# A spectral and dense block pair on one core: half of the filter rows by plain loads, x in six loads, and a new written order

## The chip, the core and the metric

The kernel runs on one core of a Trainium2 chip. The metric is the device time of one execution in microseconds; the kernel before was run three times, and its median is what a changed kernel is compared with. The profile is one execution, taken by the hardware profiler.

## What is computed

x has 2048 rows of 448 bf16 values. Two kinds of layer alternate, twice each. Layer A is a filter in frequency space; layer B is a dense layer with a squared ReLU. Both start from a layer norm and add to x:

```
def _A_ref(x, w_r, w_i):
    X = rfft2(x.astype(float32), axes=(-2, -1))
    X = X * (w_r + 1j * w_i)            # w_r, w_i: 2048 x 225
    return irfft2(X, s=(S, D), axes=(-2, -1)).astype(bfloat16)
def _B_ref(x, w1, b1, w2, b2):
    h = einsum("bsd,df->bsf", x, w1) + b1     # 448 -> 1792
    r = where(h > 0, h, 0)
    return einsum("bsf,fd->bsd", r * r, w2) + b2
x = x + _A_ref(_layernorm(x), A_w_r, A_w_i)
x = x + _B_ref(_layernorm(x), B_w1, B_b1, B_w2, B_b2)
x = x + _A_ref(_layernorm(x), A_w_r, A_w_i)
x = x + _B_ref(_layernorm(x), B_w1, B_b1, B_w2, B_b2)
```

## The kernel before

Row p*16 + t of x is partition p of tile t; there are 16 tiles of 128 x 448. The transform over the 2048 rows is split into 128 x 16, all as matmuls with constant tables:

- First stage (`first_A`, one call for each tile): a 128 x 256 table FA is scaled by the rows' 1/std into Fs (`scaled`, recorded at line 758, 760 or 762 by engine), five matmuls bring x, its mirror copy xr and the mean m2 through it, and an evacuation writes XA. xr is a reversed copy of half of each row, made by GpSimd or ACT (units "XR", line 744); it lies in the tile VT. The statistics come from `ln_stats` on VectorE (bn_stats at line 865, aggregate at 866), or, for the tiles in `ACT_STATS`, from two passes on ACT (`act_stats`, lines 887 and 888), then a square root on ACT and a reciprocal (896).
- Spectral stage (`spectral`): `stage_TD` takes the transform over the 448 columns (64 matmuls in the first layer), evacuated to U in `arena`; `stage_B` ("quad") ends the transform over the rows with the table G; its evacuation lands in EF, also in `arena`; `stage_W` multiplies with the filter Wt on VectorE (line 780, 16 products of 128 x 896, written to `wide`); `stage_Bi` ("row") starts the way back with the table H (256 matmuls, eight groups of 32) and is evacuated to VT.
- `ffn`: `stage_TI` and `stage_AI` end the way back (tables TI, FI); x is updated; `ln_B` prepares the layer norm; yT, the transposed input, comes by matmuls (`flip`) for tiles 0 and 1 and by a transposing DMA on SP for the other tiles, two at a time; `h_part` and `h_pairs` multiply with W1, `o_tile` with W2. Then `second_A` feeds the second spectral layer. All matmuls but the fillers are recorded at line 718; matmuls on `ones` at line 1375 are fillers that keep TensorE busy.

The filter tile Wt has four blocks of 16 x 225 values for each partition: rows of w_r and of w_i, and for both the mirrored rows that belong to the negative frequencies. Partition p holds in the first two blocks rows from 128*(p & 15) + 16*(p >> 5) + 1 on, 16 rows in one run of 7200 bytes. Before, all four blocks come by an indirect DMA on GpSimd's queue (`gather`, line 838), with row numbers that VectorE works out from an iota (`ints`, line 800). In GpSimd's list the two mirrored blocks are gathered first, early in the first stage; the two direct blocks (units 26 and 25) come near the end of the list, the one after the scaled tables of tiles 12 and 13, the other last before three fillers. Two small loads, tagged L.W0, write row 0 and its fellows over one row of partitions 96 to 127 of the mirrored blocks, so they need the mirrored gathers to have landed. A product needs all four blocks.

The program records units (a matmul group, an evacuation, a load) with numbers in the order in which they are created. `ORDER` holds, for each of the five engines, the list of its units in the order in which they are issued; every engine goes through its list in turn and waits for what its next unit needs. A load is a unit on the list of the queue that issues it, SP, ACT or GpSimd; a queue that waits for one unit issues nothing behind it. `_Sched.schedule` with the constants `DMA_FIRST`, `TURN`, `PACE` and so on is a model of the times; with a written ORDER it sets the filler matmuls, the banks of PSUM and on which side a wait is put, not the lists. Units that can run on ACT or VectorE run on that engine in whose list they stand.

Loads before, on SP in this order: x tile 0, FA, x tiles 2, 4, 6-7, 10-11, 14-15, TD, G, G0, the two halves of H (each waits until tile 11, or 13, of XA is evacuated), L.W0 twice, TI, FI, J, b1, b2, W1 in two loads (384 rows over 128 partitions, 64 rows over 64), b1 over two rows, TQ, W2, then the first transposing DMA. On ACT: x tiles 1, 5, 8-9, 3, 12-13.

Of the kernel before, what the change touches and what calls it, by code (L numbers as in the profile page):

```python
# [6 lines left out]
ALU = mybir.AluOpType  # L7
# [4 lines left out]
P = 128  # L12
# [21 lines left out]
def make_constants():  # L34
# [64 lines left out]

    H = np.zeros((P, 16, 2, 3, 16, 2, 2))  # L100
    for n in range(16):
        for j in range(4):
            kappa = 16 * j + n + 1
            for f in range(2):
# [10 lines left out]
                for k, M in enumerate((-s, c, s)):  # L115
                    H[32 * j:32 * j + 32, n, f, k, :, j % 2] = M
# [29 lines left out]
1275 1280 1247 1241 1291 1285 1288 1294 1297""",  # L146
    "act": """
# [11 lines left out]
1231 1179 1189 1184 1058 1187 1182 1253 1258 1256 1263 1261 1251 1266 1268 1271 1273 1276 1283 1281 1278""",  # L159
    "dve": """  # L160
# [22 lines left out]
1242 1286 1289 1295 1298""",  # L183
    "pool": """
16 0 30 28 27 46 29 31 33 54 32 34 35 109 37 99 112 36 96 26 151 138 135 25 19 17 18""",
    "sp": """
4 5 7 9 11 13 15 38 39 40 155 156 157 158 159 160 161 162 163 164 165 166 167 168 286 306 324 326 344 327 362 380 398
# [1279 lines left out]
```

## Time and profile before

| | |
|---|---|
| three runs | 259.51, 264.21, 259.23 us; median 259.51 |
| the profiled execution, its own time | 258.75 us |
| its span, first to last instruction | 257.0 us |
| granted TensorE clock | 1.000 |
| moved by DMA | 18.10 MB in 23936 packets |
| instructions | 6149, of these 2462 matmuls |

How to read it: a row of the timeline has start and duration in us, engine, line, operation, the tile that is written and the tiles that are read, how often it was repeated, and in brackets the idle time ahead of it with what ended it. A row of the groups has busy us and the mean ns of one. A row of the stages gives, for a stretch, the busy time of PE, PEld (weight load), DVE (VectorE), ACT (ScalarE) and POOL (GpSimd), the granted clock, the share of the 16 DMA engines that is busy, and GB/s. SPq and ACTq are the queues that issue loads. A row of DMA issues ends with KB and the us from issue to landing. The tile W_sb stands for W1_sb and W2_sb, since digits are left out of names.

### The profile page before, as it was taken

The numbers are of one execution on the slowest core, as the hardware profiler recorded it, in microseconds if no ns is written. First come the engines' busy times: TensorE is split into PE (matmuls) and PEld (weight loads), VectorE is DVE, ScalarE is ACT, GpSimd is POOL, SyncE is SP. The second block draws the span as 40 slices with busy tenths as digits, with TensorE's granted clock in tenths as the row PEclk, the third lists the DMA queues.
The fourth block names the chain that finished last, engine by engine and source line by source line (L and its number), as shares of the span: only waits on it lengthen the run. The fifth ranks groups of instructions, "written<-read, shape, count | busy, mean of one in ns | idle before, by whom it ended". The sixth has DMA issues, their size and how long they took to land.

```text
span 257.0 us, 6149 instructions
## 1 busy us (share of the span) xinstructions
PE 246.8 (96%) x2462; PEld 160.8 (63%) x2462; DVE 191.8 (75%) x628; ACT 168.5 (66%) x363; POOL 14.3 (6%) x31
## 2 busy tenths in 40 slices
PE   8799788999999999999999999999999999999995
PEld 2578577886544865544558778787645775545453
DVE  3994796999875759889999898999982288023732
ACT  5987888986467775207957898999368883018300
POOL 4890000000000000000000000000000000000000
PEclk9999999999999999999999999999999999999999
DMA  6989945011321000130000000022231021000025
GB/s 180 414 278 395 288 111 176 15 28 43 73 46 43 0 0 3 42 42 3 0 3 1 3 3 3 3 41 45 42 79 41 0 61 41 3 18 0 3 80 172
DMA packets 23936, 18.10 MB, mean 70 GB/s; under 512 B 15938, under 2 KB 22562, under 8 KB 23908
## 3 DMA queue, kind: packets, MB, share of 16 engines
q1 hardware_dynamic: 22612, 13.22, 18.6%
q0 software_dynamic: 576, 3.69, 3.7%
q10 hardware_dynamic: 720, 0.80, 1.0%
q8 instruction: 19, 0.31, 0.5%
q14 instruction: 9, 0.07, 0.1%
HBM read 12.20 MB, written 1.84 MB: 55 GB/s over the span
## 4 chain that ended last, share of the span: by engine, by line
PE 73%; DVE 11%; ACT 7%; DMA 6%; issue 2%; POOL 1%; SPq 0%; POOLq 0%; DVEq 0%
PE ps L718 72%; DMA Wt<-in_A_w_r_dram,ix 4%; ACT arena L743 3%; ACT VT L743 2%; DMA xin<-in_A_x_dram 2%; DVE arena L780 2%; DVE st L865 2%; DVE wide L780 1%; DVE x_sb L1228 1%; ACT arena L737 1%; PE ps L1375 1%; DVE VT L1107 1%; DVE x_sb L1082 1%; DVE Fs L758 1%; DVE wide L789 1%
## 5 line engine op out<-in xcount | busy, mean ns | idle before, releaser
L718 PE MATMUL ps<-wide,W_sb 64*128 64x512 bf16 (+1 forms) x770 | 90.1, 346 | 0.0
L718 PE MATMUL ps<-W_sb,arena 128*128 128x448 bf16 (+3 forms) x476 | 87.1, 342 | 0.0
L718 PEld LDWEIGHTS ps<-wide,W_sb 64*128 64x128 bf16 (+1 forms) x770 | 57.2, 95 | 29.3 <-issue 1.5
L737 ACT ACTIVATE arena<-ps,b1col 128x512 bf16<-128x512 f32 x84 | 52.2, 687 | 27.0 <-PE ps L718 26.8
L718 PEld LDWEIGHTS ps<-W_sb,arena 128*128 128x128 bf16 x476 | 45.5, 98 | 38.0 <-issue 0.4
L780 DVE TENSOR_TENSOR arena<-arena 128x512 bf16<-128x512 bf16 (+1 forms) x140 | 45.1, 365 | 24.5 <-ACT arena L737 24.4
L1106 ACT ACTIVATE VT<-x_sb 128x448 bf16<-128x448 bf16 x28 | 16.2, 581 | 13.3 <-DVE x_sb L1082 13.3
L743 ACT ACTIVATE arena<-ps 128x896 bf16<-128x896 f32 (+1 forms) x27 | 20.5, 828 | 3.7 <-PE ps L718 3.6
L780 DVE TENSOR_TENSOR wide<-arena,Wt 128x896 bf16<-128x896 bf16 x32 | 17.7, 617 | 1.9 <-DMA Wt<-in_A_w_r_dram,ix 1.9
L737 ACT ACTIVATE arena<-ps 128x256 bf16<-128x256 f32 x56 | 17.9, 400 | 1.8 <-PE ps L718 1.3
L737 ACT ACTIVATE mv<-mv,epst 128x1 f32<-128x1 f32 (+1 forms) x45 | 12.6, 294 | 9.4 <-DVE mv L866 8.1
L1228 DVE SCALAR_TENSOR_TENSOR x_sb<-ps,mv,xin 128x448 bf16<-128x448 f32 (+2 forms) x13 | 8.1, 643 | 14.1 <-PE ps L718 14.0
L718 PE MATMUL ps<-H_sb,wide 64*128 64x128 bf16 x512 | 16.2, 217 | 1.2 <-issue 1.2
L743 ACT ACTIVATE XA<-ps 128x512 bf16<-128x512 f32 (+1 forms) x28 | 14.3, 581 | 4.2 <-PE ps L718 4.1
L718 PEld LDWEIGHTS ps<-H_sb,wide 64*128 64x128 bf16 x512 | 14.4, 94 | 4.0 <-issue 2.2
L718 PE MATMUL ps<-wide,VT 64*128 64x512 bf16 x42 | 15.8, 377 | 0.0
L743 ACT ACTIVATE wide<-ps 128x896 bf16<-128x896 f32 (+3 forms) x19 | 13.9, 780 | 1.9 <-PE ps L718 1.9
L743 ACT ACTIVATE VT<-ps 128x1024 bf16<-128x1024 f32 (+1 forms) x16 | 12.7, 876 | 1.6 <-PE ps L718 1.5
L1375 PE MATMUL ps<-ones 128*128 128x512 bf16 (+2 forms) x32 | 10.3, 450 | 2.9 <-DVE m L879 1.3
L744 DVE CAST arena<-ps 128x896 bf16<-128x896 f32 (+1 forms) x11 | 9.3, 873 | 5.0 <-PE ps L718 5.0
L762 ACT ACTIVATE wide<-x_sb,rstd 128x448 bf16<-128x448 bf16 x12 | 8.1, 675 | 6.6 <-DMA wide<-wide 5.1
L1082 DVE SCALAR_TENSOR_TENSOR x_sb<-ps,mv,xin 128x448 bf16<-128x448 f32 x16 | 10.5, 678 | 0.4 <-PE ps L718 0.3
(83 smaller groups left out, 277.7 us busy)
## 6 DMA issues: line engine op xcount, KB each, us to landing
out_dram<-x_sb SPq DMA_DIRECT2D x15, 112.0 KB, 1.8
W_sb<-in_B_w_dram SPq DMA_DIRECT2D x1, 1568.0 KB, 8.1
H_sb<-c_H SPq DMA_DIRECT2D x2, 768.0 KB, 8.1
W_sb<-in_B_w_dram SPq DMA_DIRECT2D x1, 1344.0 KB, 11.3
xin<-in_A_x_dram SPq DMA_DIRECT2D x3, 224.0 KB, 5.6
G_sb<-c_G SPq DMA_DIRECT2D x1, 512.0 KB, 10.7
xin<-in_A_x_dram ACTq DMA_DIRECT2D x2, 224.0 KB, 5.0
VT<-in_B_w_dram SPq DMA_DIRECT2D x2, 192.0 KB, 3.1
```

The source lines that it names most:

```text
L718: return sch.add("pe", lambda e: e.matmul(_res(o), lhsT, rhs, start=start, stop=stop, skip_group_check=skip), [lhsT, rhs], [o], cost=cost, ...
L737: sch.add("act", lambda e: e.activation(o, _res(i), func, **kw), rd, [o], cost=c)
L743: op = sch.add(engs[0], lambda e: e.activation(o, _res(i), ACT.Copy) if h[0].eng == "act" else e.tensor_copy(o, _res(i)), [i], [o], cost=c ...
L744: e.tensor_copy(o, _res(i)), [i], [o], cost=c[engs[0]], unit=unit)
L758: return e.tensor_scalar(o, i, s, 1.0, op0=ALU.mult, op1=ALU.mult)
L762: op = sch.add(engs[0], lambda e: e.activation(o, i, ACT.Copy, scale=s) if h[0].eng == "act" else scale(e), [i, s], [o], cost=c[engs[0]])
L780: sch.add(eng, lambda e: e.tensor_tensor(o, _res(a), b, op), [a, b], [o], cost=_free(o) / rate + 69.0)
L865: small(lambda e, si=si, xi=xi: e.bn_stats(si, xi), [xi], [si], _free(xi) / 0.96 + 69.0)
L1082: small(lambda e, xx=xx, xi=xi, r=r, m=m: e.scalar_tensor_tensor(out=xx, in0=_res(r), scalar=m, in1=xi, op0=ALU.subtract, op1=ALU.add), [r ...
L1106: op = sch.add("act", lambda e, i=i, o=o, x=x, h=h: e.activation(o, x, ACT.Square, accum_out=sd[:, i, 1:2]) if h[0].eng == "act" else e.sc ...
L1228: small(lambda e: e.scalar_tensor_tensor(out=o, in0=_res(i), scalar=rs[0] if rs else 1.0, in1=xi, op0=ALU.add if t >= 4 and last else ALU. ...
L1375: return lambda e: e.matmul(ps[:, b, 0:n], ones[:], ones[:, None, :].to_broadcast([P, n // P, P]), start=True, stop=True)
```

## The change

1. Two gathers instead of four. The direct blocks of the filter come by eight plain loads on SP, one for each of four groups of 32 partitions and each of w_r, w_i, behind G0. For this partition p now holds the rows of (p & 30) >> 1 instead of p & 15, and the tables G, G0 and H are permuted alike (`by`); the two L.W0 loads have a source of [16 rows][2][225] instead of [2][16 rows][225].
2. The two halves of H no longer wait for XA: they follow the plain filter loads at once.
3. x comes in six loads instead of eleven: tiles 0, 4-7 and 12-15 on SP, 1, 2-3 and 8-11 on ACT.
4. Tiles 3 and 5 get their statistics on VectorE; tiles 2-3 and 4-5 are groups of two. Only tile 1 stays with ACT.
5. New lists for all engines, and other constants in the model.

There are six units fewer ahead of the spectral stage, so a unit that was number n is now n - 6 from old number 171 on. Some units of the new lists: 11 ones, 12 the filler memset of W1, 0 iota, 19 and 20 the gathers (w_r, w_i), 21 to 29 the mirror copies of tiles 0, 1, 2-3, 4-5, 6-7, 8-9, 10-11, 12-13, 14-15; 64, 67, 77, 90, 93, 103, 106, 129, 132, 119, 142, 145 the scaled tables of tiles 2, 3, 4, 6, 7, 8, 9, 12, 13, 11, 14, 15; 30 to 32 TD, G, G0; 33 to 40 the plain filter loads; 149 and 150 H; 151 and 152 L.W0; 153 to 159 TI, FI, J, b1, b2, W1; 160 b1 over two rows; 280 the first transposing DMA; 161 TQ; 162 W2.

```diff
+    by = [16 * r + k for k in range(16) for r in range(2)]
+    G, G0 = (M.reshape(M.shape[:-1] + (2, 32))[..., by].reshape(M.shape) for M in (G, G0))
...
-                    H[32 * j:32 * j + 32, n, f, k, :, j % 2] = M
+                    H[32 * j:32 * j + 32, n, f, k, :, j % 2] = M[by]
...
     "pool": """
-16 0 30 28 27 46 29 31 33 54 32 34 35 109 37 99 112 36 96 26 151 138 135 25 19 17 18""",
+11 12 0 23 20 21 24 29 25 67 64 90 93 77 28 27 103 106 129 132 13 119 142 145 19 14""",
     "sp": """
-4 5 7 9 11 13 15 38 39 40 155 156 157 158 159 160 161 162 163 164 165 166 167 168 286 306 324 326 344 327 362 380 398
...
+4 5 8 10 30 31 32 33 34 35 36 37 38 39 40 149 150 151 152 153 154 155 156 157 158 159 160 280 161 162 300 318 320 338
...
-A1GROUPS = ((0, 1), (1, 1), (2, 1), (3, 1), (4, 1), (5, 1), (6, 2), (8, 2), (10, 2), (12, 2), (14, 2))
-ACT_STATS = (1, 3, 5)
+A1GROUPS = ((0, 1), (1, 1), (2, 2), (4, 2), (6, 2), (8, 2), (10, 2), (12, 2), (14, 2))
+ACT_STATS = (1,)
...
-    DMA_FIRST = 3500.0
-    TURN = 100.0
+    DMA_FIRST = 2900.0
+    TURN = 93.0
...
+    FETCH = (94, 128, 4300.0)
...
-        row = ((0, 2, 15, ALU.bitwise_and, 7, ALU.logical_shift_left), (1, 2, 5, ALU.logical_shift_right, 4, ALU.logical_shift_left))
+        row = ((0, 2, 30, ALU.bitwise_and, 6, ALU.logical_shift_left), (1, 2, 5, ALU.logical_shift_right, 4, ALU.logical_shift_left))
...
-        for a, n, q in ((0, 1, "sp"), (1, 1, "act"), (2, 1, "sp"), (3, 1, "act"), (4, 1, "sp"), (5, 1, "act"), (6, 2, "sp"),
-                        (8, 2, "act"), (10, 2, "sp"), (12, 2, "act"), (14, 2, "sp")):
+        for a, n, q in ((0, 1, "sp"), (1, 1, "act"), (2, 2, "act"), (4, 4, "sp"), (8, 4, "act"), (12, 4, "sp")):
             dma(q, xin[:, a:a + n, :], x_dram[:, a:a + n, :])
...
-        ints(ix[:, 0:1], ix[:, 2:3], 1, ALU.bitwise_or, 0, ALU.bitwise_or)
-        ints(ix[:, 1:2], ix[:, 2:3], 2032, ALU.bitwise_xor, 0, ALU.bitwise_or)
+        ints(ix[:, 0:1], ix[:, 2:3], 2032, ALU.bitwise_xor, 0, ALU.bitwise_or)
...
         for w in range(2):
-            gather(0, w, WS * w, 16)
-        sch.tag = "M2"
-        for w in range(2):
-            gather(1, w, WS * (2 + w), 16)
+            gather(w, WS * (2 + w), 16)
...
         dma("sp", G0_sb[:], dc["G0"])
+        for j in range(4):
+            for w, a in enumerate((A_w_r, A_w_i)):
+                sch.tag = f"L.W.{j}.{w}"
+                dma("sp", Wt[32 * j:32 * j + 32, WS * w:WS * (w + 1)],
+                    bass.AP(a.tensor, a.offset + (16 * j + 1) * (LW + 1), [[P * (LW + 1), 16], [0, 2], [1, WS]]))
...
-            dma("sp", H_sb[:, 8 * i:8 * i + 8], dc["H"][:, 8 * i:8 * i + 8], after=[XA[:, 0, 0, 0, 11 + 2 * i, 0:1]])
+            dma("sp", H_sb[:, 8 * i:8 * i + 8], dc["H"][:, 8 * i:8 * i + 8])
         for w, a in enumerate((A_w_r, A_w_i)):
             sch.tag = f"L.W0.{w}"
             dma("sp", Wt[96:128, WS * (2 + w):WS * (2 + w) + LW + 1],
-                bass.AP(a.tensor, a.offset, [[0, 2], [P * (LW + 1), 16], [1, LW + 1]]))
+                bass.AP(a.tensor, a.offset, [[P * (LW + 1), 16], [0, 2], [1, LW + 1]]))
```

More of the change, by code (lines that the diff above doesn't have):

```diff
@@ L136 @@
     "pe": """
[9 rows of a table removed]
-1275 1280 1247 1241 1291 1285 1288 1294 1297""",
-    "act": """
[11 rows of a table removed]
-1231 1179 1189 1184 1058 1187 1182 1253 1258 1256 1263 1261 1251 1266 1268 1271 1273 1276 1283 1281 1278""",
-    "dve": """
[22 rows of a table removed]
-1242 1286 1289 1295 1298""",
[9 rows of a table added]
+1274 1235 1241 1232 1282 1279 1285 1288 1291""",
+    "act": """
[11 rows of a table added]
+1252 1255 1257 1262 1250 1260 1272 1277 1270 1267 1275 1265""",
+    "dve": """
[22 rows of a table added]
+1283 1280 1286 1289 1292""",
     "pool": """
-16 0 30 28 27 46 29 31 33 54 32 34 35 109 37 99 112 36 96 26 151 138 135 25 19 17 18""",
+11 12 0 23 20 21 24 29 25 67 64 90 93 77 28 27 103 106 129 132 13 119 142 145 19 14""",
     "sp": """
-4 5 7 9 11 13 15 38 39 40 155 156 157 158 159 160 161 162 163 164 165 166 167 168 286 306 324 326 344 327 362 380 398
-948 969 987 989 990 1007 1025 1043 1152 1061 1193 1243 1155 1293 1199 1196 1202 1240 1146 1149 1290 1287 1246 1249
-1296 1299""",
+4 5 8 10 30 31 32 33 34 35 36 37 38 39 40 149 150 151 152 153 154 155 156 157 158 159 160 280 161 162 300 318 320 338
+321 356 374 392 942 963 981 983 1001 984 1143 1140 1019 1037 1055 1240 1149 1190 1193 1237 1243 1234 1281 1284 1287
+1146 1196 1187 1290 1293""",
 }
@@ L400, in schedule @@
         begun = [0.0] * self.DEEP
-        sent = 0.0
+        sent, block = 0.0, 0.0
         def supply(start):
-            nonlocal sent
+            nonlocal sent, block
             sent = max(sent + self.PACE, begun[-self.DEEP])
+            if (len(begun) - self.DEEP) % self.FETCH[1] == self.FETCH[0]:
+                block = sent = max(sent, block + self.FETCH[2])
             start = max(start, sent)
@@ L433, in ready_of @@
                             same = d.eng == u.eng and not d.is_dma
-                            r = max(r, done[d] + d.lat + (40.0 if u.eng == "pe" else 0.0) - off)
+                            r = max(r, done[d] + (50.0 if d.is_dma and d.cost != 1000.0 else d.lat) + (40.0 if u.eng == "pe" else 0.0) - off)
                     off += op.cost
@@ L469, in schedule @@
         total = len(self.units)
-        mode = "full"
+        mode, turn = "full", self.TURN
         avail = {}
@@ L487, in schedule @@
                         if u.mode != mode:
-                            f += self.TURN
+                            f += turn
                     starts.append((max(r, f), u))
@@ L530, in schedule @@
                     free["pe"] += unit
-                start = max(start, free["pe"] + (self.TURN if u.mode != mode else 0.0))
+                start = max(start, free["pe"] + (turn if u.mode != mode else 0.0))
                 mode = u.mode
@@ L566, in schedule @@
             if e == "pe":
+                turn = self.TURN + u.ops[-1].lat - 200.0
                 used.append((start, t))
@@ L711, in dma @@
                 w = min(run(o), run(i))
-                sch.add(eng, fn, reads, writes, is_dma=True, cost=450.0 if o.tensor.name not in onchip else 550.0, lat=n / w * (7.5 + 2.0 * w / 27.0) / 16.0 * (2.0 if writes and _parts(o) == 64 else 1.0))
+                sch.add(eng, fn, reads, writes, is_dma=True, cost=460.0, lat=n / w * (7.5 + 2.0 * w / 27.0) / 16.0 * (2.0 if writes and _parts(o) == 64 else 1.0))
         def mm(o, lhsT, rhs, start, stop, skip=False, unit=None):
@@ L815, in bass_interleave_layers__spectral_gfnet__dense_activation_squared_relu__prompt_kernel @@
         act(warm[:, 0:1], warm[:, 0:1], ACT.Sqrt)
+        sch.units[-1].ops[0].cost = 1300.0
         sch.table_deps = [sch.last_write[k] for k in _pages(warm[:, 0:1])][:1]
-        for a, n, q in ((0, 1, "sp"), (1, 1, "act"), (2, 1, "sp"), (3, 1, "act"), (4, 1, "sp"), (5, 1, "act"), (6, 2, "sp"),
-                        (8, 2, "act"), (10, 2, "sp"), (12, 2, "act"), (14, 2, "sp")):
+        for a, n, q in ((0, 1, "sp"), (1, 1, "act"), (2, 2, "act"), (4, 4, "sp"), (8, 4, "act"), (12, 4, "sp")):
             dma(q, xin[:, a:a + n, :], x_dram[:, a:a + n, :])
@@ L832, in bass_interleave_layers__spectral_gfnet__dense_activation_squared_relu__prompt_kernel, with gather @@
         sch.add("dve", lambda e: e.tensor_tensor(ix[:, 2:3], ix[:, 0:1], ix[:, 1:2], ALU.bitwise_or), [ix[:, 0:2]], [ix[:, 2:3]], cost=75.0)
-        ints(ix[:, 0:1], ix[:, 2:3], 1, ALU.bitwise_or, 0, ALU.bitwise_or)
-        ints(ix[:, 1:2], ix[:, 2:3], 2032, ALU.bitwise_xor, 0, ALU.bitwise_or)
-        def gather(c, w, a, n):
+        ints(ix[:, 0:1], ix[:, 2:3], 2032, ALU.bitwise_xor, 0, ALU.bitwise_or)
+        def gather(w, a, n):
             o = Wt[:, a:a + n * (LW + 1)]
-            sch.add("pool", lambda e: e.indirect_dma_start(o, None, (A_w_r, A_w_i)[w], bass.IndirectOffsetOnAxis(ix[:, c:c + 1], 0)),
-                    [ix[:, c:c + 1]], [o], is_dma=True, cost=1150.0, lat=160.0 * n)
+            sch.add("pool", lambda e: e.indirect_dma_start(o, None, (A_w_r, A_w_i)[w], bass.IndirectOffsetOnAxis(ix[:, 0:1], 0)),
+                    [ix[:, 0:1]], [o], is_dma=True, cost=1150.0, lat=160.0 * n)
         sch.bias, sch.tag = PR["M"], "M"
         for w in range(2):
-            gather(0, w, WS * w, 16)
-        sch.tag = "M2"
-        for w in range(2):
-            gather(1, w, WS * (2 + w), 16)
+            gather(w, WS * (2 + w), 16)
         for a in range(0, NT, 2):
@@ L855, in bass_interleave_layers__spectral_gfnet__dense_activation_squared_relu__prompt_kernel @@
         dma("sp", G0_sb[:], dc["G0"])
+        for j in range(4):
[3 more added lines that the diff above has]
+                    bass.AP(a.tensor, a.offset + (16 * j + 1) * (LW + 1), [[P * (LW + 1), 16], [0, 2], [1, WS]]))
+        sch.tag = ""
         def ln_stats(ts_, mean=False):
```

84 rows, old and new, of the table ORDER are left out of this document.

## The prediction

> **What bounds the kernel now.** I read the page's head first, then the chain of waits, then the first 60 us by stage and engine.
>
> ```profile
> span 257.0 us, 6149 instructions
> PE 246.8 (96%) x2462; PEld 160.8 (63%) x2462; DVE 191.8 (75%) x628; ACT 168.5 (66%) x363; POOL 14.3 (6%) x31
> ```
>
> ```profile
> 17.06 10.02 DMA Wt<-in_A_w_r_dram,ix
> ...
> 45.66 73.05 PE ps L718 x543
> ...
> 164.31 89.89 PE ps L718 x677
> ```
>
> From 45.66 us on, 163 us of the chain are two unbroken runs of TensorE; there the change only permutes orders. What it can win lies ahead of 45.66. There the chain passes the fourth filter gather, which lands at 27.08, and earlier a load of x (its waits stand below). The bytes by stage (last columns: granted clock, DMA share, GB/s):
>
> ```profile
> 0.00:5.00 5.00, 4.00 (x10) 1.45 (x11) 1.24 (x8) 2.96 (x7) 1.81 (x8) 1.00 0.56 133
> 5.00:10.00 5.00, 3.55 (x19) 1.26 (x17) 4.11 (x20) 3.89 (x14) 3.50 (x8) 1.00 1.04 391
> ...
> 15.50:16.00 0.50, 0.50 (x7) 0.44 (x6) 0.50 (x4) 0.50 (x2) 0.49 (x2) 1.00 0.00 0
> ```
>
> The transfers run full from 5 us on, yet at 15.5 they stand still while half the filter and all of H are still outside. What that costs shows on TensorE and VectorE:
>
> ```profile
> 18.86 4.76 PE L718 MATMUL ps<-TD_sb,XA 128*128 128x224 bf16 x48 [0.32 <-DVE XA L744]
> 23.55 1.33 PE L718 MATMUL ps<-arena,G_sb 64*64 64x448 bf16 x26
> ...
> 34.77 3.75 PE L718 MATMUL ps<-H_sb,wide 64*128 64x128 bf16 x128 [0.66 <-issue]
> 39.04 0.49 PE L718 MATMUL ps<-H_sb,wide 64*128 64x128 bf16 x11 [0.53 <-issue]
> ```
>
> ```profile
> 22.12 1.09 DVE L744 CAST arena<-ps 128x896 bf16<-128x896 f32 x1 [3.08 <-PE ps L718]
> ...
> 27.16 0.63 DVE L780 TENSOR_TENSOR wide<-arena,Wt 128x896 bf16<-128x896 bf16 x1 [1.88 <-DMA Wt<-in_A_w_r_dram,ix]
> ...
> 31.38 5.99 DVE L780 TENSOR_TENSOR wide<-arena,Wt 128x896 bf16<-128x896 bf16 x11
> ```
>
> The forward transform starts at 18.86 (call this T0) and the last inverse matmul ends at 39.53, 20.7 us later. VectorE idles 1.88 us before its first filter product; from that product to the last inverse matmul it is 12.37 us.
>
> **Head: x, statistics, first stage.** Five x loads fall away. Tiles 2-3 now come second on ACT's queue, tiles 4-7 third on SP's. With equal shares for both queues tiles 2-3 are in after 0.67 MB, by the rows above at 5.0 us (133 GB/s x 5), and tiles 4-7 after 1.25 MB, at 6.5 (5.0 + 0.58/0.391). Before:
>
> ```profile
> 5.44 0.63 DVE L865 BATCH_NORM_STATS2 st<-xin 128x6 f32<-128x448 bf16 x1 [1.49 <-DMA xin<-in_A_x_dram]
> ...
> 6.64 0.63 DVE L865 BATCH_NORM_STATS2 st<-xin 128x6 f32<-128x448 bf16 x1 [0.45 <-DMA xin<-in_A_x_dram]
> ```
>
> VectorE's two waits, 1.94 us, shrink to some 1.3. Its work changes by two more statistics and, by the new lists, two fewer full casts of XA:
>
> ```profile
> L758 POOL TENSOR_SCALAR Fs<-FA_sb,rstd 128x256 bf16<-128x256 bf16 x9 | 4.2, 472 | 1.2 <-DVE m L879 1.2
> ...
> L744 POOL COPY VT<-xin 128x448 bf16<-128x448 bf16 x7 | 3.7, 549 | 0.0
> L744 DVE CAST XA<-ps 128x512 bf16<-128x512 f32 x5 | 3.5, 705 | 0.4 <-PE ps L718 0.4
> ```
>
> Plus 2 x 0.63 (the rows above), minus 2 x 0.705: nothing. GpSimd is the tighter one. Its new list puts the first gather behind the mirror copy of tiles 2-3 and the mirror copy of tiles 14-15 ahead of that of 6-7 and of the scaled tables of tiles 3, 2, 6, 7, 4; so those wait for the last x load, 1.9 MB, at about 8.3 us. Then two copies of 0.55 and five tables of 0.47 put tile 4 on TensorE at 11.7, and eleven tiles of five matmuls, some 0.57 a tile (0.099 of a TD matmul, above, x 256/224 columns x 5), end at 17.9. With the 0.32 that TensorE waited for the last cast T0 is 18.2, 0.65 us earlier; bounds 17.5 (x lands sooner) and 18.9 (no gain). The filler memset of W1 now stands before the iota, 0.86 us on GpSimd (row below). VectorE's index arithmetic waits for the iota and the first statistic is queued behind it, but that ends near 2 us, when by the rows above hardly a byte of x is in: nothing; without that cover it would be 0.86. ACT loses two pairs of passes and gains two mirror copies: off the path.
>
> **Filter.** The two direct gathers go; eight plain loads of 230 KB follow G and G0 on SP, then H at once. SP issues them in about 10 us, well ahead of the bytes, so the issue is hidden by the full ring. Bytes to move until the plain rows are in: x and FA 1.90, TD and G 0.82, plain 1.84, the first gather 0.92 MB, less 0.67 moved by 5.0: 4.8 MB at 391 GB/s, 17.3 us; H, 1.57 MB, by 21.3. That needs the rate of loads over 128 partitions; these write 32 each. The nearest row is W1's 64-partition tail, which by its place in the ring moved at about 31 us; the row ahead of it is a load over all partitions:
>
> ```profile
> 30.00:31.00 1.00, 0.99 (x34) 0.82 (x35) 1.00 (x3) 0.81 (x2) 0.00 (x0) 1.00 1.05 430
> 31.00:32.00 1.00, 1.00 (x28) 0.75 (x32) 1.00 (x3) 0.92 (x2) 0.00 (x0) 1.00 0.82 179
> ```
>
> Per busy share that is 410 against 218 GB/s. At 218 the plain rows take 8.5 instead of 4.7 us and land at 21. I take the slower; H is then in at 25, still ahead of its first use at 27.8 (below). [...]
>
> The last to land is another: the second remaining gather. It stays at the end of GpSimd's list, behind the tables of tiles 14 and 15, so it is issued at about 17.4 instead of 17.06. Before, the same kind issued at 14.39 took 5.5 us and the one at 17.06 took 10.0, beside H and a stream of small loads on SP's ring:
>
> ```profile
> 14.39 1.07 POOL L838 DMA_INDIRECT Wt<-in_A_w_i_dram,ix  x1 [0.16 <-PE ps L718]
> ...
> 18.32 0.86 POOL L793 MEMSET W_sb<- 128x896 f32 x1
> ```
>
> ```profile
> Wt<-in_A_w_i_dram,ix POOLq DMA_INDIRECT x1, 5.5
> ```
>
> Now SP cannot stream beside it. The two small row loads behind H (L.W0) write into what the gathers write, so SP waits at the first of them until the gather has landed, and TI, FI, J, the biases and W1 queue behind it. Beside the gather is only the tail of H. I take 6.5 us: 23.9, bounds 22.9 and 27.4. The loads behind then start 4 to 5 us later than before: TI in at 29 (needed at 37), W1 at 35 (needed at 44). Covered.
>
> When is the filter needed? The new TensorE list runs five groups of TD (32 x 0.099 = 3.2 us), then four quads of B (34 x 0.051), ending T0 + 5.0. VectorE starts on them half a microsecond before that and has to cast B2 (1.09) and half each of B0 and B14 before its first product: T0 + 6.8 = 25.0. So the wait of 1.88 goes. TensorE's inverse starts after five products (0.545 each), at T0 + 9.6, and runs eight groups at 4.27 us per 128 matmuls (34.77 to 39.04, the pause by "issue" included) and two quads: 9.5. It ends at T0 + 19.1 = 37.3, or 12.3 us after the filter's landing if that is later. Against 39.53 this is 2.2 us.
>
> **Given back.** In SP's new list the load of W2 and TQ stand behind the first transposing DMA. Before:
>
> ```profile
> 46.54 4.09 PE L718 MATMUL ps<-wide,W_sb 128*128 128x256 bf16 x36
> ...
> 59.75 2.81 PE L718 MATMUL ps<-W_sb,arena 128*128 128x448 bf16 x14
> ```
>
> ```profile
> 49.70 1.34 SPq L705 DMA_TRANSPOSE wide<-x_sb  x1
> ```
>
> ```profile
> W_sb<-in_B_w_dram SPq DMA_DIRECT2D x1, 1568.0 KB, 8.1
> ```
>
> The transpose goes out 3.2 us after the first product with W1, takes SP 1.3, TQ's issue I take as 0.4; W2 lands 8.1 after its issue: 13.0, or up to 13.9 if the transpose's inputs come later in VectorE's new list. It is needed after 13.2. I take 0.3 us; bounds 0 and 1.2. Nothing but TensorE itself hides it.
>
> The order behind: unit numbers from 165 on are the old ones less six, and TensorE's list moves them by 0.6 to 4.7 places on average. VectorE's moves by 5 to 30, with some 40 evacuations exchanged with ACT, but in 45.66 to 118.7 and 164.3 to 254.2 TensorE never waits. Zero, bounds -1 and +1.
>
> **Sum.** 0.65 from T0 and 1.55 from the filter stage, less 0.3: 1.9 us off the profiled execution, 258.75 to 256.85. The median of the runs was 259.51, 0.76 above it, so 257.6.
>
> **The rivals.**
> 1. The last gather still lands late, near the 10.0 us row: at 27.4 the inverse ends at 39.7, and with W2 the time is 260.0. For it: the gather is issued no earlier than before and meets H, if the plain rows are slow. Against: the ring behind H stands still. Chance 0.2.
> 2. W2 decides: SP's transpose comes 1 us later and W2 lands 1.2 us after it is needed: 258.5. For it the bounds above; against it that the lead already is 13.0 against 13.2. Chance 0.12.
> 3. The other side, slower: the eight loads of 32 partitions run at a quarter (109 GB/s, the 64-partition row halved again). They take 16.9 us from about 12.6 and land at 29.5, and H behind them in the same ring at 33.3. The last product then waits; the inverse ends 12.3 after 29.5, 41.8, plus 0.3 for W2: 262.1. It decides from the point where a plain row lands after 27. Against it: only that 64 partitions reach 218. Chance 0.07.
> 4. The permuted order saves too in the middle (between the two long runs, 118.7 to 164.3 us, where VectorE and ACT share the chain): 1 us more, 256.6. Chance 0.13.
> 5. The plain loads aren't worth anything, since the wait only moves: VectorE's products start at 25 but TensorE is held by H or evacuations as before; only T0 and W2 count: 259.2. Chance 0.08.
>
> **How the numbers follow.** My forecast has 0.4, with its own range 256.8 to 258.4. All terms at their best: 1.35 from T0, 1.55, 1 from the order, 3.9 in all: 255.6. A late gather and a late W2 together: 260.9. The range 255.5 to 260.9 leaves out the third rival and little more. About 2% is what a measurement of this kernel can tell from no change: under 254.3 would need 5.2 us and only the whole head could give that (0.03); over 264.7 needs the third rival and more (0.04); within, 0.93.
>
> **What would show it.** Right: no hole in the transfers between 14.5 and 17 us; VectorE's first filter product at about 25 with no DMA before it; the gather in under 7 us and SP idle at the row loads until it lands; TD from 18.2, inverse ended at about 37.3; the first product with W2 without a wait over 0.5. Wrong: a wait of L780 on a plain row, TensorE waiting for H_sb, the first stage's end later than 18.5, or a gain that appears after 45 us instead of before.

## The result and the profile after

| | before | changed |
|---|---|---|
| runs | 4, median 259.37 us (258.72 to 264.21) | 4, median 266.21 us (265.74 to 267.27) |
| profiled execution | 258.75 us, span 257.0 | 266.51 us, span 264.7 |

The ratio is 1.0278, 95% interval [1.0233, 1.0323]: slower by 2.8%, 6.8 us between the medians, where 257.6 (255.5 to 260.9) was predicted. Ratios here and below leave disturbed runs of both kernels out.

The chain of waits of the changed kernel (start, duration, what) says where the time went. VectorE's first filter product starts at 33.82; the prediction had 25.0 and the kernel before 27.16:

```profile
4.82 12.34 DMA Wt<-in_A_w_r_dram
17.17 0.56 SPq L716
17.78 4.02 DMA Wt<-in_A_w_i_dram
21.81 7.88 DMA Wt<-in_A_w_i_dram
29.71 3.94 DMA Wt<-in_A_w_i_dram
33.82 2.25 DVE wide L786 x4
```

The chain runs through plain filter loads, one after another. SP's own queue shows the issues, H and a row-0 load (L.W0) behind them:

```profile
4.82 0.81 SPq L716 DMA_DIRECT2D Wt<-in_A_w_r_dram  x1
5.68 0.58 SPq L716 DMA_DIRECT2D Wt<-in_A_w_i_dram  x1
17.17 0.56 SPq L716 DMA_DIRECT2D Wt<-in_A_w_r_dram  x1
...
20.76 0.56 SPq L716 DMA_DIRECT2D Wt<-in_A_w_r_dram  x1
...
28.90 0.56 SPq L716 DMA_DIRECT2D Wt<-in_A_w_r_dram  x1
29.71 0.56 SPq L716 DMA_DIRECT2D Wt<-in_A_w_i_dram  x1
30.31 1.06 SPq L716 DMA_DIRECT2D H_sb<-c_H  x2
31.41 0.57 SPq L716 DMA_DIRECT2D Wt<-in_A_w_r_dram  x1
```

Two loads go out, then SP stands from 6.3 to 17.17. The third is issued when the first has landed, the fifth when the third has, and so on: not eight issues in 10 us, but 25.5 us from the first to the last. The cause is in the program. Its tracker of dependencies, `_pages`, names what a load writes by tensor and column and ignores partitions. The four loads of w_r write the same columns of four partition groups, so the program takes each for a second write of what the one before wrote, and makes SP wait for its landing.

What TensorE and VectorE do meanwhile (rows of the timeline, then of the stages):

```profile
20.91 3.23 PE L724 MATMUL ps<-TD_sb,XA 128*128 128x224 bf16 x32 [0.32 <-issue]
...
36.12 5.30 PE L724 MATMUL ps<-H_sb,wide 64*128 64x128 bf16 x96 [6.27 <-DVE wide L786]
...
43.70 3.97 PE L724 MATMUL ps<-H_sb,wide 64*128 64x128 bf16 x136 [0.57 <-issue]
```

```profile
8.08 1.15 DVE L873 BATCH_NORM_STATS2 st<-xin 128x6 f32<-128x448 bf16 x2 [2.37 <-DMA xin<-in_A_x_dram]
...
33.82 3.85 DVE L786 TENSOR_TENSOR wide<-arena,Wt 128x896 bf16<-128x896 bf16 x7 [6.60 <-DMA Wt<-in_A_w_i_dram]
```

```profile
10.00:15.00 5.00, 4.51 (x28) 3.29 (x29) 4.53 (x23) 3.88 (x10) 4.91 (x11) 0.66 0.97 271
15.00:18.50 3.50, 3.50 (x35) 3.13 (x32) 2.55 (x14) 2.68 (x7) 1.65 (x5) 1.00 0.10 26
...
26.50:30.00 3.50, 3.35 (x42) 2.59 (x40) 0.72 (x2) 3.50 (x6) 0.00 (x0) 1.00 0.06 16
35.00:40.00 5.00, 3.88 (x74) 3.88 (x76) 3.59 (x7) 0.84 (x2) 0.00 (x0) 0.50 0.89 280
40.00:45.00 5.00, 4.43 (x115) 3.59 (x111) 4.49 (x9) 3.75 (x5) 0.00 (x0) 0.85 0.72 266
```

The hole in the transfers that the change should have closed is now two holes, 15 to 18.5 and 26.5 to 30. TensorE waits 6.27 us and then begins the inverse at a granted clock of 0.50; it ends at 47.67 instead of 39.53. The first stage is late too: it ends at 20.91 (before 18.86), VectorE having waited 2.37 us for tiles 4 to 7, with a clock of 0.66 from 10 to 15. From the first product with W1 (54.46, before 46.54) to the end of the span both executions take nearly the same, 210.2 and 210.5 us: the loss lies wholly ahead of it.

### The profile page after: what moved, and what is told of

It is laid out like the page before. It is cut to its first block, busy times and chain, and to the rows that moved or that the text cites. A ratio compares the mean times of both kernels' runs of the same rounds, so it can differ in the third digit from the quotient of the medians.

```text
span 264.7 us, 6125 instructions
## 1 busy us (share of the span) xinstructions
PE 248.7 (94%) x2459; PEld 155.9 (59%) x2459; DVE 194.5 (73%) x629; ACT 163.6 (62%) x350; POOL 13.0 (5%) x30
## 4 chain that ended last, share of the span: by engine, by line
PE 75%; DMA 11%; ACT 6%; DVE 5%; SPq 2%; issue 1%; DVEq 0%
PE ps L724 74%; DMA Wt<-in_A_w_i_dram 6%; DMA Wt<-in_A_w_r_dram 5%; ACT arena L749 4%; ACT VT L749 2%; SPq L716 2%; DVE wide L786 1%; DVE x_sb L1090 1%; DVE wide L750 1%; PE ps L1383 0%; DVE x_sb L1236 0%; DVE VT L1115 0%; DVE st L873 0%; DVE VT L750 0%; DVE Fs L764 0%
## 5 line engine op out<-in xcount | busy, mean ns | idle before, releaser
L724 PEld LDWEIGHTS ps<-wide,W_sb 64*128 64x128 bf16 (+1 forms) x770 | 50.3, 95 | 37.1 <-issue 1.3
L724 PE MATMUL ps<-H_sb,wide 64*128 64x128 bf16 x512 | 17.8, 234 | 6.8 <-DVE wide L786 6.3
L724 PEld LDWEIGHTS ps<-H_sb,wide 64*128 64x128 bf16 x512 | 16.7, 104 | 8.3 <-DVE wide L786 6.7
L743 ACT ACTIVATE mv<-mv,epst 128x1 f32<-128x1 f32 (+1 forms) x43 | 11.8, 293 | 13.0 <-DVE mv L874 12.7
L749 ACT ACTIVATE XA<-ps 128x512 bf16<-128x512 f32 (+1 forms) x29 | 15.1, 595 | 4.6 <-PE ps L724 4.6
L749 ACT ACTIVATE VT<-ps 128x1024 bf16<-128x1024 f32 (+1 forms) x15 | 11.8, 888 | 8.3 <-PE ps L724 8.3
L749 ACT ACTIVATE wide<-ps 128x896 bf16<-128x896 f32 (+2 forms) x19 | 13.6, 756 | 2.5 <-PE ps L724 2.5
L1383 PE MATMUL ps<-ones 128*128 128x512 bf16 (+2 forms) x29 | 9.0, 415 | 5.0 <-DVE rstd L904 2.2
L873 DVE BATCH_NORM_STATS2 st<-xin 128x6 f32<-128x448 bf16 x15 | 8.8, 609 | 3.2 <-DMA xin<-in_A_x_dram 3.2
L1090 DVE SCALAR_TENSOR_TENSOR x_sb<-ps,mv,x_sb 128x448 bf16<-128x448 f32 x16 | 10.5, 676 | 0.3 <-PE ps L724 0.2
```

The source lines that it names most:

```text
L724: return sch.add("pe", lambda e: e.matmul(_res(o), lhsT, rhs, start=start, stop=stop, skip_group_check=skip), [lhsT, rhs], [o], cost=cost, ...
L743: sch.add("act", lambda e: e.activation(o, _res(i), func, **kw), rd, [o], cost=c)
L749: op = sch.add(engs[0], lambda e: e.activation(o, _res(i), ACT.Copy) if h[0].eng == "act" else e.tensor_copy(o, _res(i)), [i], [o], cost=c ...
L873: small(lambda e, si=si, xi=xi: e.bn_stats(si, xi), [xi], [si], _free(xi) / 0.96 + 69.0)
L1090: small(lambda e, xx=xx, xi=xi, r=r, m=m: e.scalar_tensor_tensor(out=xx, in0=_res(r), scalar=m, in1=xi, op0=ALU.subtract, op1=ALU.add), [r ...
L1383: return lambda e: e.matmul(ps[:, b, 0:n], ones[:], ones[:, None, :].to_broadcast([P, n // P, P]), start=True, stop=True)
```

## The experiments

Each version computes all that the kernel before does. T0 is the start of the first TD matmul, the product is VectorE's first with the filter; both in us from one profiled execution each.

| run | T0 | product | median us | ratio to before |
|---|---|---|---|---|
| changed kernel | 20.91 | 33.82 | 266.21 | 1.0278 [1.0233, 1.0323] |
| e1_free_rows | 24.59 | 32.56 | 264.66 | 1.0162 [1.0055, 1.0269] |
| e2_free_rows_w2 | 20.29 | 30.48 | 266.72 | 1.0261 [1.0159, 1.0364] |
| e3_before_h_first | 19.96 | 27.81 | 262.61 | 1.0104 [1.0061, 1.0146] |
| e4_fillers | 22.45 | 31.68 | 264.57 | 1.0169 [1.0080, 1.0258] |
| e5_x_by_two | 21.08 | 33.59 | 264.90 | 1.0206 [1.0150, 1.0261] |
| e6_free_rows_after_x | 22.34 | 30.86 | 262.35 | 1.0125 [1.0059, 1.0190] |
| e7_before_rows_chain | 19.95 | 29.79 | 263.11 | 1.0151 [1.0096, 1.0206] |
| e8_before_rows | 19.11 | 25.66 | 258.13 | 0.9953 [0.9925, 0.9980] |
| e9_before_rows_row0 | 19.80 | 26.14 | 258.72 | 0.9976 [0.9951, 1.0000] |
| e10_before_x6 | 20.45 | 28.96 | 259.72 | 1.0025 [1.0005, 1.0045] |
| e11_free_rows_x11 | 20.12 | 30.84 | 262.78 | 1.0149 [1.0116, 1.0183] |
| e12_gathers_first | 19.91 | 27.55 | 258.30 | 0.9992 [0.9957, 1.0026] |

**The chain taken out of the changed kernel.**

```diff
 def _pages(ap):
...
+    if name == "Wt":
+        p = ap.offset // row
+        return [(name, j, int(i)) for j in range(p // 32, (p + pat[0][1] - 1) // 32 + 1) for i in pg]
     return [(name, int(i)) for i in pg]
```

> The changed kernel, with one thing undone: the program's own tracker of what a unit must wait for now tells the four groups of 32 partitions of Wt apart, so that a plain load of one group no longer waits for the landing of the load of another group. Theory (the chain of landings): the eight loads go out one behind the other by about 10 us, SP does not stand until the row loads behind H, the first filter product comes at 26 to 28 us (the second gather, issued at 19.8, is the last to land) instead of 33.8, and the time is 258.5 to 261. Rival (loads of 32 partitions are slow in themselves, or the gather is slowed by them): the products still start after 31 and the time stays above 264. Either way the first stage stays late: TD starts near 20.9.

264.66 us. In this run's trace SP issues as the prediction said (last plain load at 9.92, H right behind), but the rest of the theory misses:

```profile
9.92 0.59 SPq L719 DMA_DIRECT2D Wt<-in_A_w_i_dram  x1
10.55 1.06 SPq L719 DMA_DIRECT2D H_sb<-c_H  x2
```

```profile
10.00:15.00 5.00, 3.33 (x14) 1.87 (x15) 4.68 (x23) 2.45 (x6) 2.82 (x6) 0.50 1.06 269
15.00:20.00 5.00, 5.00 (x29) 3.67 (x27) 2.09 (x9) 2.62 (x7) 3.46 (x9) 0.57 1.05 232
```

```profile
23.50 1.02 POOL L846 DMA_INDIRECT Wt<-in_A_w_r_dram,ix  x1 [0.15 <-issue]
```

The transfers are busy throughout, at 232 GB/s where loads over all partitions moved 416 (10 to 15 us in e8). The first stage crawls at a granted clock of 0.50 and 0.57 in these rows and ends at 24.59, so GpSimd, whose list has the last gather behind the scaled tables, issues it at 23.50 only. So the chain was one limit, and a second stood close behind it. How late the first stage is varies from one execution to the next: the four runs of e1 took 263.28 to 266.46 us, the profiled one 266.02, and e2, which has the same code up to there, issues this gather at 19.21 and has T0 at 20.29.

**W2 forward too.** As e1, with TQ and W2 ahead of the first transposing DMA on SP.

```diff
-158 159 160 280 161 162 300
+158 159 161 162 160 280 300
```

> As the run before, with TQ and W2 put ahead of the first transposing DMA in SP's list, as in the kernel before. In the changed kernel W2 landed at 68.7 and the first product with it began at 68.79, with no idle time on TensorE. If the place of W2 costs nothing, this is within 0.5 us of the run before it; if W2 is late once the filter is early, it is 0.5 to 1.2 us faster.

266.72 us; no gain, so the place of W2 costs nothing here. That W2 forward harms is not shown: the intervals of e1 and e2 overlap. TensorE stands within the inverse, some seven matmuls before its end, with no wait that the profile shows ("issue"), while W1's tail and W2 fill the transfers (243 GB/s from 42.5 to 46); e1 has a pause at the same place, of 2.12 us:

```profile
46.27 0.40 PE L727 MATMUL ps<-H_sb,wide 64*128 64x128 bf16 x7 [3.73 <-issue]
```

**H alone.** The kernel before, with H not waiting for XA.

```diff
-dc["H"][:, 8 * i:8 * i + 8], after=[XA[:, 0, 0, 0, 11 + 2 * i, 0:1]])
+dc["H"][:, 8 * i:8 * i + 8])
```

> The kernel before with one part of the change alone: the two halves of H no longer wait for XA and go out behind G0, all else as before. Theory: the hole in the transfers at 15 to 17 us closes, the last gather (issued at 17.06) finds less beside it, lands at 23 to 25 instead of 27.08, the wait of 1.88 us ahead of the first product goes, and the time is 257.3 to 258.3. Rival: what then streams behind H on SP's ring (TI, W1) slows the gather as much as H did, it lands at 27 again and the time is 259.0 to 259.8.

262.61 us, slower by 1.0%. The hole is closed (from 15 to 20, 416 GB/s) and nothing is won: T0 is 1.1 us later than before, the last gather is issued 0.8 us later and takes 9.9, and TensorE has a longer pause by "issue":

```profile
15.00:20.00 5.00, 4.23 (x42) 3.49 (x42) 4.59 (x15) 4.69 (x11) 4.66 (x8) 1.00 1.03 416
```

```profile
27.81 0.63 DVE L780 TENSOR_TENSOR wide<-arena,Wt 128x896 bf16<-128x896 bf16 x1 [1.43 <-DMA Wt<-in_A_w_r_dram,ix]
```

```profile
41.35 0.83 PE L718 MATMUL ps<-H_sb,wide 64*128 64x128 bf16 x23 [1.92 <-issue]
```

**The clock.** The changed kernel with its chain; the model of times is told that the last plain loads land 3.5 us later each, so it puts 25 filler matmuls into TensorE's wait.

```diff
                     bass.AP(a.tensor, a.offset + (16 * j + 1) * (LW + 1), [[P * (LW + 1), 16], [0, 2], [1, WS]]))
+                if j == 3:
+                    sch.units[-1].ops[0].lat += 3500.0
```

> The changed kernel with the chain of landings left as it is, but with 25 filler matmuls (about 5.4 us) ahead of the first inverse group, where TensorE stood for 6.3 us; the model's time of the last two plain loads is set later for that, nothing else. If the granted clock falls because TensorE stood, the clock stays at 1.00 in the stage from 35 to 45 us, the inverse takes about 10 us instead of 11.6 from its first matmul to its last, and the time falls by 1.5 to 2.5 us, to about 264. If the clock falls for another reason, or does not matter, the time stays at 266.

264.57 us, 1.6 less than the changed kernel. With the clock at 1.00 the inverse, 36.84 to 45.31, takes 8.5 us; in the changed kernel 36.12 to 47.67, 11.5:

```profile
36.84 2.85 PE L724 MATMUL ps<-H_sb,wide 64*128 64x128 bf16 x96
40.67 4.64 PE L724 MATMUL ps<-H_sb,wide 64*128 64x128 bf16 x160
```

So the half clock went with TensorE's wait, and with fillers in the wait the clock stayed at 1.00. That they win the time is not shown. The inverse ends 2.36 us earlier than in the changed kernel, but in this execution the last plain load came earlier, and the first product already starts 2.14 us earlier:

```profile
31.68 3.85 DVE L786 TENSOR_TENSOR wide<-arena,Wt 128x896 bf16<-128x896 bf16 x7 [2.91 <-DMA Wt<-in_A_w_i_dram]
```

From the product to the end of the inverse it is 13.63 us here and 13.85 in the changed kernel: the fillers run until 36.84, and what the clock wins behind them they had taken before.

**The size of the x loads.** The changed kernel, loads of four tiles split into two of two.

```diff
+            u = sch.new_unit(q)
+            for b in range(a, a + n, 2):
+                dma(q, xin[:, b:min(b + 2, a + n), :], x_dram[:, b:min(b + 2, a + n), :], unit=u)
```

> The changed kernel, each x load of four tiles split into two of two tiles on the same queue, the chain of landings kept. Theory (the size of the loads makes the head late): the first stage's end moves from 20.9 to 19 to 19.5 us, but the filter still waits for the chain, so the time gains at most 1 us: 265 to 266.5. Rival (what is queued in the ring behind x makes it late, not the size): the first stage's end stays at 20.5 or later and the time at 266 to 267.

264.90 us. The first stage ends at 21.08, so smaller loads alone do not mend the head. But the run does not settle the size of a load. VectorE's new list takes tiles 6 and 7 (units 83 and 85) ahead of 5 and 4 (72 and 70), so what it waits for until 8.78 is the second half of the split load. The first half was in by 7.66, when GpSimd copies tiles 4 and 5; whole, the load came at 8.08:

```profile
8.78 1.15 DVE L875 BATCH_NORM_STATS2 st<-xin 128x6 f32<-128x448 bf16 x2 [3.02 <-DMA xin<-in_A_x_dram]
```

```profile
7.66 0.56 POOL L750 COPY VT<-xin 128x448 bf16<-128x448 bf16 x1 [1.04 <-DMA xin<-in_A_x_dram]
```

The ratio is 0.7% lower than the changed kernel's; the two intervals overlap.

**Plain loads after x.** As e1; each plain load waits until x is in.

```diff
-[[P * (LW + 1), 16], [0, 2], [1, WS]]))
+[[P * (LW + 1), 16], [0, 2], [1, WS]]), after=[xin[:, 4:5, :], xin[:, 8:9, :], xin[:, 12:13, :]])
```

> The changed kernel without the chain of landings, and the first plain filter load waits on SP until x has landed. Theory (the plain loads at half rate in the ring beside x made the run without the chain so late): the first stage ends at 19.5 to 21 instead of 24.6 us, the plain rows land by 21, the last gather is issued at 18.5 to 19.5 and lands at 27.5 to 28.5, the first product follows at once; 260 to 262 us. Rival (the x loads themselves are late, whatever follows them): the first stage ends after 23 us, the time stays at 263.5 to 266.

262.35 us. The time is nearly what the theory said, its steps are not: T0 is 22.34, and VectorE waits for tiles 4 to 7 until 9.55 although no plain load is beside x. So these loads are not what delays x. What decides is again the last gather:

```profile
21.26 1.03 POOL L846 DMA_INDIRECT Wt<-in_A_w_r_dram,ix  x1
```

Issued at 21.26 and 9.3 us under way, it lands at 30.5, and the first product follows at 30.86.

**The rows alone, with the chain and without.** The kernel before with the plain rows in place of the two direct gathers (loads start when x is in); all else is old, the other two gathers stand early in GpSimd's list as before.

```diff
-            gather(0, w, WS * w, 16)
+                dma("sp", Wt[32 * j:32 * j + 32, WS * w:WS * (w + 1)],
+                    bass.AP(a.tensor, a.offset + (16 * j + 1) * (LW + 1), [[P * (LW + 1), 16], [0, 2], [1, WS]]),
+                    unit=two[j // 2], after=[xin[:, 12:13, :], xin[:, 14:15, :]])
...
-4 5 7 9 11 13 15 38 39 40 155 156
+4 5 7 9 11 13 15 38 39 40 25 26 155 156
```

> The kernel before with the first part of the change alone: no direct gathers, the eight plain loads behind G0, the rows permuted; the loads start when x is in and wait for one another's landing as in the change. Old loads of x, old statistics, old order. Theory (each link costs 4 us or more on SP, and H is queued behind): last plain rows at 25 to 28, H issued after 21 and landed after 27; 260 to 262.5 us. Rival (with x left alone, the chain hides behind the first stage): no later than 259.5.

> As the run of the kernel before with plain rows, but the eight loads do not wait for one another. Theory (what was lost came from the chain and from x; half the rows by plain loads are worth having by themselves): first stage ends at 18 to 18.9 us, all plain rows in by 22, H by 26, the first product at 25 to 25.7 behind no load, 257 to 258.7 us. Rival (the half rate of loads to 32 partitions costs what the two gathers cost, or more): the first product waits for a plain row or TensorE waits for H, 259.5 to 262.

263.11 with the chain, 258.13 without: the chain alone is worth 5.0 us here. With it, SP's issues and the first product:

```profile
9.66 0.71 SPq L712 DMA_DIRECT2D Wt<-in_A_w_r_dram  x1
...
26.23 0.56 SPq L712 DMA_DIRECT2D Wt<-in_A_w_i_dram  x1
26.84 1.06 SPq L712 DMA_DIRECT2D H_sb<-c_H  x2
```

```profile
29.79 0.63 DVE L782 TENSOR_TENSOR wide<-arena,Wt 128x896 bf16<-128x896 bf16 x1 [3.42 <-ACT arena L745]
```

(The last wait is put down to ACT, but the last plain load, issued at 26.23 with a median of 3.6 us to landing, is what came at 29.8.) Without it:

```profile
9.75 0.71 SPq L715 DMA_DIRECT2D Wt<-in_A_w_r_dram  x1
...
14.31 0.65 SPq L715 DMA_DIRECT2D Wt<-in_A_w_i_dram  x1
17.55 1.29 SPq L715 DMA_DIRECT2D H_sb<-c_H  x2
```

```profile
10.00:15.00 5.00, 4.98 (x45) 3.71 (x43) 5.00 (x27) 5.00 (x17) 4.76 (x11) 1.00 1.05 416
15.00:20.00 5.00, 4.64 (x48) 3.94 (x47) 3.89 (x13) 3.88 (x9) 2.65 (x6) 1.00 1.02 210
```

```profile
25.66 0.63 DVE L785 TENSOR_TENSOR wide<-arena,Wt 128x896 bf16<-128x896 bf16 x1
...
30.34 0.63 DVE L785 TENSOR_TENSOR wide<-arena,Wt 128x896 bf16<-128x896 bf16 x1 [1.44 <-DMA Wt<-in_A_w_i_dram]
```

The first product waits for no load and starts 6.55 us after T0. H came later than the theory had it: TensorE waits 0.53 us for it at 29.79. This is the one version whose whole interval lies below the kernel before: 1.4 us less in the medians, ratio 0.9953.

**Row 0 ahead of H.** The wait of 1.44 us at 30.34 is for L.W0, which came in 11 us after its issue, behind H.

```diff
-40 25 26 155 156 157 158 159
+40 25 26 157 158 155 156 159
```

> As the run of the kernel before with plain rows that do not wait for one another, with the two small loads of row 0 (L.W0) ahead of H on SP instead of behind it. Theory (VectorE's wait of 1.44 us at 30.3 was for these, 11 us in a full ring behind H): they land by 25, that wait goes, and the time falls by 0.5 to 1.2 us to 257.0 to 257.7. Rival (H's second half, for which TensorE waited 0.53 us at 29.8, or the casts take the wait over): no gain over 0.3, 257.9 to 258.4.

258.72 us. The wait is gone, the gain is not there: T0 was 0.7 later (the lists are the same until SP's load at 14 us), and TensorE pauses by "issue" instead:

```profile
34.75 4.07 PE L723 MATMUL ps<-H_sb,wide 64*128 64x128 bf16 x139 [1.36 <-issue]
```

Its interval [0.9951, 1.0000] overlaps that of e8; the two can't be told apart.

**x alone.** The kernel before with its x in six loads.

```diff
-        for a, n, q in ((0, 1, "sp"), (1, 1, "act"), (2, 1, "sp"), (3, 1, "act"), (4, 1, "sp"), (5, 1, "act"), (6, 2, "sp"),
-                        (8, 2, "act"), (10, 2, "sp"), (12, 2, "act"), (14, 2, "sp")):
+        for a, n, q in ((0, 1, "sp"), (1, 1, "act"), (2, 2, "act"), (4, 4, "sp"), (8, 4, "act"), (12, 4, "sp")):
```

> The kernel before with its x in the six loads of the change, nothing else (old statistics, old order, four gathers). Theory (the six loads by themselves bring tiles 4 to 7 late, at 8 us or later, since loads in one ring land together): TensorE pauses over 2 us early in the first stage, the first stage ends at 20 to 20.8 instead of 18.9, 260.3 to 262. Rival (the late head comes from the new order and statistics): first stage ends at 19.2 or earlier, 259 to 260.

259.72 us; the ratio of 1.0025 is 0.65 us. T0 moved as the theory said (20.45), the time as the rival said. The theory's ground, that loads in one ring land together, the changed kernel shows for some: G, G0 and the first two plain loads, issued on SP from 3.07 to 5.68, landed from 16.5 to 17.7. The x loads of tiles 4-7 and 12-15, issued at 1.65 and 2.12, landed there at 8.05 and 9.72, and here that of tiles 4-7 was in by 7.60, not at 8 or later. In the profiled executions the pauses by "issue" in the inverse (1.19 us in the kernel before) were not there, and from the first product to the end of the inverse it is 11.16 us where it was 12.37; that makes up for most of T0:

```profile
20.45 4.76 PE L718 MATMUL ps<-TD_sb,XA 128*128 128x224 bf16 x48 [0.32 <-DVE XA L744]
...
34.22 5.90 PE L718 MATMUL ps<-H_sb,wide 64*128 64x128 bf16 x192
```

**All but the x loads.** As e6, with the eleven x loads of before.

> The changed kernel with plain loads that start when x is in and do not wait for one another, and with the eleven x loads of before; new order and statistics. Theory (the x loads were what made this kernel's first stage late): first stage ends at 18.5 to 19.3, the last gather is issued by 18 and lands at 26 to 28, 259 to 261 us. Rival (the order and the two more statistics on VectorE): first stage ends at 20.5 or later, 261.5 to 263.

262.78 us, the rival's time; T0, 20.12, lies between the two. Neither had the reason: the time is that of e6, because the gather, issued at 19.04, now takes 11.5 us beside the plain rows and H. TensorE waits for the product that waits for it:

```profile
33.14 4.48 PE L727 MATMUL ps<-H_sb,wide 64*128 64x128 bf16 x96 [4.07 <-DVE wide L789]
```

**The gather.** As e11, the second gather right behind the first in GpSimd's list.

```diff
-16 17 0 28 25 26 29 34 30 72 69 95 98 82 33 32 108 111 134 137 18 124 147 150 24 19
+16 17 0 28 25 24 26 29 34 30 72 69 95 98 82 33 32 108 111 134 137 18 124 147 150 19
```

> As the run of the changed kernel with free plain loads after x and the eleven x loads of before, with the second gather right behind the first in GpSimd's list instead of last. Theory (what is left of the loss is this gather, issued at 19.0 us and 11.5 us under way beside the plain rows and H, while VectorE and TensorE wait 4.4 and 4.1 us): issued by 8 and landed by 18, the plain rows are the last of the filter at 23 to 25, the first product runs at 26.5 to 27.5 without a load ahead of it, 258.5 to 260 us. Rival (the plain rows or H end just as late, or the new order itself is slow): the first product or the inverse still waits over 2 us, 261 us or more.

258.30 us, 0.9992 [0.9957, 1.0026]: all of the loss is gone, though the new order, the new statistics and the new place of W2 are still there. The product starts at 27.55, behind the last plain load; that wait of 1.33 us the theory did not have, nor one of 1.03 us of TensorE for H at 29.89:

```profile
27.55 3.85 DVE L789 TENSOR_TENSOR wide<-arena,Wt 128x896 bf16<-128x896 bf16 x7 [1.33 <-DMA Wt<-in_A_w_i_dram]
```

```profile
7.95 0.94 POOL L847 DMA_INDIRECT Wt<-in_A_w_r_dram,ix  x1 [0.30 <-issue]
```

## Why the prediction was wrong

**The step that failed** is "SP issues them in about 10 us, well ahead of the bytes, so the issue is hidden by the full ring." The loads wait for one another, and their issue took 25.5 us from the first to the last. That wait stands in `_pages`, which the diff does not touch. I counted issues and bytes, and did not ask of each new load what the tracker would make it wait for. e7 against e8 prices that alone at 5.0 us. In the changed kernel the last plain row lands at 33.7 in place of 21, and H is issued at 30.31, in place of landing at 25.

**The gather, second.** "I take 6.5 us: 23.9" was wrong as well, hidden behind the chain. Its issue was 19.83, not 17.4, since it stands behind the last scaled tables, which wait for VectorE's statistics (1.06 us at 18.74), and it took 9.3. From e11 to e12 its place is worth 1.6% (1.0149 to 0.9992), some 4 us. From the changed kernel to e6, the chain gone and the loads behind x, it is another 1.5%. With the x loads, which make no difference here (e6 to e11, 1.0125 to 1.0149), these steps take in the whole loss. Neither was enough alone: with both gathers early the chain still leaves a loss of 1.5% (e7), and without the chain the gather is the next limit (it lands at 30.5 in e6 and e11). The first rival had this mechanism; it priced it against a prompt filter.

**T0.** 18.2 was forecast, 20.91 came. VectorE could begin on tiles 4 to 7 at 8.08; 6.5 was forecast. TensorE then had 0.22 us of work from 7.0 to 9.4, and later the clock fell:

```profile
7.00:9.40 2.40, 0.22 (x2) 0.00 (x0) 1.32 (x5) 0.00 (x1) 0.56 (x1) 1.00 1.02 391
...
12.00:13.00 1.00, 1.00 (x7) 0.69 (x6) 1.00 (x6) 0.54 (x2) 1.00 (x3) 0.50 0.96 259
```

So the late head was paid for twice, in the wait and in matmuls at half speed (one every 0.21 us at 12.5, every 0.11 at 15). Of the change's parts, the six loads cost 0.65 us by themselves (e10). They need not be the only reason: e12, with eleven loads and the clock at 1.00 throughout the first stage, has T0 at 19.91, and VectorE waits for tiles 6 and 7 until 8.62. So the new lists, which ask for these tiles first, or the two more statistics, put down as "nothing", may delay T0 too; with the scatter told below one execution does not show it.

**The given-back term and the order behind** lay within their bounds. W2 cost 0 (0.3 forecast, bounds 0 to 1.2), if barely: in the changed kernel the first product with it starts at 68.79, and it landed at 68.7. e12, with the whole new order, equals the kernel before. **The rate** was right: 218 GB/s was taken for loads over 32 partitions, 210 was measured at a busy share of 1.02, where loads over all partitions moved 416 at 1.05 (e8).

**The rivals.** The third, slower, had the right event, a plain row landing after 27, with the wrong mechanism (a quarter of the rate; it is half, 210 against 416). Its price, 12.3 us from the last landing to the end of the inverse, is 13.9 here (33.82 to 47.67), with the inverse begun at a granted clock of 0.50. With 0.07 for it and 260.9 as the top, the range left out what happened.

**What stays open.** Where x lands is not settled. VectorE waited for the load of tiles 4 to 7 until 8.08 in the changed kernel, 9.82 in e4 and 9.33 in e1, 8.28 in e2, and each pair has the same code up to there; T0 differs by 1.5 and 4.3 us between them. With the old lists the same load was in by 7.60 (e10). Plain loads beside x are not the reason (e6), e5 leaves the size of a load open, and no experiment separated the order of the queues.

## What to carry to other kernels

A transfer that is split by partitions is checked against the program's own tracker of dependencies: if that knows only columns, the pieces wait for one another's landing, and everything behind them on the queue waits too (here 25.5 us from the first issue to the last, with H behind). When several loads must all land before one product, the last to land sets the time, so a load that is long under way goes out first: in e11 that was the gather, issued at 19.04 and 11.5 us under way, and its early place in e12 is worth some 4 us. And a hole in the transfers is no evidence that filling it helps: e3 filled it and lost 1% (1.0104).

## What the runs showed of the hardware

- The granted clock was 1.00 or 0.50 in the half-microsecond rows of the changed kernel, e1, e2 and e3; the few rows between the two (0.52 to 0.91) are stretches in which it changed. In the first stage of the changed kernel it was 0.50 for some 3 us, after a gap of 2.20 us without work on TensorE, and in e1 over all of 10 to 15 us. Less work on TensorE did not by itself bring the lower clock: in e12 it was busy 1.98 of the 5 us from 5 to 10 and the clock stayed at 1.00, in e11 3.32 and the clock was 0.94 there and 0.72 from 10 to 15. What sets it is not shown.
- TensorE's pauses by "issue" within the inverse came in most kernels at one of two places: about 120 matmuls into it (the kernel before, the changed kernel, e12) or seven to eleven before its end (the kernel before again, e1, e2, e6, e11). Between the two pauses of the kernel before stand 128 matmuls. What the pauses are is not shown.
- The pauses' length differs, and the traffic beside them alone does not explain it: 0.66 and 0.53 us in the kernel before, the first while nothing moved (0 GB/s) and the second at 373 GB/s; 1.92 in e3 (290 falling to 20 GB/s in the half-microsecond rows from 39.5 to 41), 2.30 in e6 (89 GB/s from 40 to 45, around it) and 3.73 in e2 (243 GB/s from 42.5 to 46). Whether loads beside them make them longer was not tested.
- A gather of one filter block (128 rows of 7200 bytes) took 8.8, 10.0, 5.5 and 10.0 us in the kernel before, 11.7 and 9.3 in the changed kernel, and 11.5 for the last one in e11, where the plain rows and H moved beside it (271 GB/s in all from 19 to 25 us).
